# Two FNet and MLP layers on one core: two subtractions from GpSimd to VectorE, stores and raw loads issued later

## The chip, the core and the metric

The kernel runs on one core of a Trainium2 chip. The core's engines are named here as in the profile: PE (TensorE, the matmuls; PEld is its loading of the stationary operand), DVE (VectorE), ACT (ScalarE), POOL (GpSimd) and SP (SyncE, which in this kernel does nothing but issue DMA transfers, all of them, in one order). Matmul results go to PSUM, which has eight banks; everything else lies in SBUF, or in DRAM. The metric is device microseconds of one execution of the whole program, the median of several.

## The reference

S = 2048 tokens, D = 576 features, F = 4608 hidden features, fp32. Two layers with the same weights:

```python
x = A_x
x = x + _A_ref(_layernorm(x), seq_re, seq_im, hid_re, hid_im)
x = x + _B_ref(_layernorm(x), w1, b1, w2, b2)
x = x + _A_ref(_layernorm(x), seq_re, seq_im, hid_re, hid_im)
x = x + _B_ref(_layernorm(x), w1, b1, w2, b2)

def _A_ref(x, seq_re, seq_im, hid_re, hid_im):      # y = Re(DFT_seq(DFT_hidden(x)))
    a = einsum("bsd,ed->bse", x, hid_re)
    b = einsum("bsd,ed->bse", x, hid_im)
    return einsum("ts,bse->bte", seq_re, a) - einsum("ts,bse->bte", seq_im, b)

def _B_ref(x, w1, b1, w2, b2):
    h = gelu(einsum("bsd,df->bsf", x, w1) + b1)
    return einsum("bsf,fd->bsd", h, w2) + b2
```

## The kernel before

**Precision and parts.** An fp32 matrix is used as the sum of two fp32r matrices, a high and a low part: ACT copies the value to fp32r (the high part), and DVE or POOL subtracts that from the value (the low part). A product takes three matmuls: high by high, high by low, low by high (`PASSES`). On top of that every product is a two-by-two block product in Strassen's manner (Winograd's form): seven products in place of eight, numbered 1 to 7, each of a sum of blocks of one matrix by a sum of blocks of the other. "Part 6 of w1" is the sum of blocks that enters product 6, split in high and low.

**Stages.** Per layer: the transform (layer norm and both Fourier matrices), then the MLP in two passes of 1024 tokens each. There are four MLP passes; the change concerns the first one (layer 0, first half of the tokens, some 470 to 920 us into the span) and the transform ahead of it (94 to 390 us), since only there the parts of w1 and w2 are computed. Each part is stored to DRAM (`w1_parts`, `w2_parts`; the profile's queries shorten both to `w_parts`). w1's parts are loaded back in the pass itself; all later passes load both.

**One group of the first pass.** The hidden features go in 36 blocks of 128, taken in pairs q = 0 to 17, and two pairs make a group g = 0 to 8. The loop over g (the last lines of `mlp`) runs

- the *first inner*: `inner(2g)`, w1 by the tokens for a pair: seven steps, one for each part in the order 1, 6, 2, 5, 7, 3, 4 (`ORDER`), seven matmuls of 128x512 each. DVE and ACT combine the products in PSUM and apply the GELU; what comes out is H, whose own seven parts are made by `step(n)`, a few instructions at a time, behind the next matmuls (`work`);
- the *first outer*: `outer` for the parts 1, 6, 5, 3 of group g-1: H by w2, 96 matmuls of 128x288. A part is done in two halves of 512 tokens, each in a PSUM bank pair of its own: 1 and 6, 5 and 3, 7 and 4 follow one another in the same banks, so the first matmul of a half waits until DVE has added the half of the part before to the sums in SBUF;
- the *second inner*: `inner(2g+1)`;
- the *second outer*: parts 7, 4, 2 of group g-1, 72 matmuls.

So a group is 266 matmuls. Group 9 (the "last group") has no inner, only the outer work of group 8; in it the transform of the next tokens already starts to load (x, `uv_mid`, `dh_mid`: the "dh loads").

**w1's parts** are made by `weights()`: for each pair q seven steps n, each with a high part (`high(n)`, two ACT instructions), one pump later its low part (`low(n)`, DVE), a store (the "w1 store") and, where a raw block was used for the last time, the load of the same block of the next pair (a "raw load": a22, a21, a11, a12 in this order). The parts lie in `stage`, a ring of three slots: `high(n)` writes the slot that the store of n-3 reads. One `pump()` is one step; in the first pass `tick` calls it after every second inner step, so that a group sees seven pumps, three in the first inner and four in the second. w1 is complete after group 6. In the profile's rows a w1 store is `w_parts<-R` from a 128x640 piece (320 KB), a raw w1 load `A<-in_w` 192 KB.

**w2's parts** are made in the pass by `make(g)`, for the outer work of the same group: raw blocks b11, b12, b22, b21 and a sum x lie in one tile `rv`; four subtractions (b12-b11, b22-x, b21-x, b22-b12) give the other sums, all on POOL. For each part a function `hi` (ACT) and a function `lo` (DVE, then the store of 576 KB) stand in the list `due` with a position: `advance()` is called behind every inner step (positions 0 to 6 and 15 to 21) and every half part of the outer work (7 to 14), and runs what is due. Some `lo` are followed by the load of a raw block of the next group (288 KB, `A<-in_w` too).

**Loads of weights.** `load_w` at each inner step takes the next w1 part into one of the slots `c1`, some four or five steps ahead of its use (320 KB, `R<-w_parts`).

**Order.** Every engine runs its instructions in the order in which the code emits them. SP issues each transfer when its source is ready and its target free, and everything behind it waits as long; no more than eight transfers are under way at a time, since the n-th waits for the one eight places ahead of it to land. ACT and PE have the same instructions in the same order before and after.

Lines named in the rows: L187 `dma`, L190 `add`, L193 `sub`, L200 `mm`, L266 and L267 `high`, L941 `hi`, L997 the GELU, L1024 the copy behind product 1, L1057 H's high parts, L717 a high part of the transform.

Of the kernel before, what the change touches and what calls it, by code (L numbers as in the profile page):

```python
# [1 line left out]

# [6 lines left out]
F32 = mybir.dt.float32  # L9
# [8 lines left out]
DH = D // 2  # L18
NP = NT // 2
NQ = F // P // 2  # L20
# [133 lines left out]
def spectral_mixer(ctx: ExitStack, tc: tile.TileContext, x, dh, c0, cs, w1, b1, w2, b2, out):  # L154
# [8 lines left out]
    nc = tc.nc  # L163
# [6 lines left out]
    w1s = nc.dram_tensor("w1_parts", (NQ, 7, P, 5 * P), F32, kind="Internal").ap()  # L170
    w2s = nc.dram_tensor("w2_parts", (NG, 7, P, 2, 2 * DH), F32, kind="Internal").ap()
# [12 lines left out]
    middle = const.tile([P, 1], F32, name="middle")  # L184

    def dma(dst, src):
        nc.sync.dma_start(dst, src)  # L187

    def add(engine, dst, a, b, op=OP.add):
        engine.tensor_tensor(dst, a, b, op=op)  # L190

    def sub(engine, dst, a, b):
        engine.tensor_tensor(dst, a, b, op=OP.subtract)  # L193
# [52 lines left out]
    def weights():  # L246
        b = raw(4, 3 * P)
        a22, a21, a11, a12 = (b[:, k] for k in range(4))
        g = nc.gpsimd
        steps = ((4, a22, lambda: add(g, a22, a21, a22)), (1, a11, lambda: sub(g, a21, a11, a21)),  # L250
                 (5, a22, lambda: sub(g, a11, a22, a11)), (2, a12, lambda: sub(g, a12, a12, a11)),
                 (7, a21, None), (6, a11, None), (3, a12, None))

        def load(q, k):
            if q < NQ:
                dma(b[:, k], w1[q][:, k])

        def at(n):
            return stage(3, 5 * P)[:, n % 3]

        def cut(a):
            return a.rearrange("p (k f) -> p k f", f=P)

        def high(n):
            src, t = cut(steps[n % 7][1]), cut(at(n))
            nc.scalar.activation(t[:, 1:4:2], src[:, 0:3:2], AF.Copy)  # L266
            nc.scalar.activation(t[:, 2], src[:, 1], AF.Identity, bias=power[:, 2:3], scale=middle)  # L267

        def low(n):

            q, k = divmod(n, 7)
            i, src, then = steps[k]
            t = cut(at(n))
            sub(nc.vector, t[:, 0:5:2], cut(src), t[:, 1:4].bitcast(F32))
            dma(w1s[q, i - 1], at(n).bitcast(F32))
            if then:
                then()
            if k in (2, 4, 5, 6):
                load(q + 1, (2, 4, 5, 6).index(k))
            if k == 6:  # L280
                made[0] = q + 1

        for k in range(4):
            load(0, k)
        yield
        for n in range(7 * NQ + 1):
            if n:
                low(n - 1)
            if n < 7 * NQ:
                high(n)  # L290
            yield
        stage.free()
        raw.free()
# [20 lines left out]
    class Sequence:  # L314
# [228 lines left out]
        def sums(self, t):  # L543
            add(nc.vector, self.tmp(NP, P), self.block(t, 2), self.block(t, 3))
            sub(nc.vector, self.block(t, 2), self.block(t, 2), self.block(t, 0))
# [349 lines left out]
    def mlp(hid, store, first, after):  # L895
# [10 lines left out]
        got1, got2 = {}, {}  # L906
# [19 lines left out]
        due = []  # L926
# [4 lines left out]
        def load_raw(g, k):  # L931
            if g < NG:
                dma(rv[:, k], w2[2 * g:2 * g + 2, :, k].rearrange("f p d -> p f d"))

        def make(g):
            b11, b12, b22, b21, x = (rv[:, k] for k in range(5))
            pool = nc.gpsimd

            def hi(i, src):
                got2[g, i] = c2.take()  # L940
                nc.scalar.activation(got2[g, i](2, 2, DH)[:, :, 0], src, AF.Copy)  # L941

            def lo(i, src):
                t = got2[g, i](2, 2, DH)
                sub(nc.vector, t[:, :, 1], src, t[:, :, 0].bitcast(F32))
                dma(w2s[g, i - 1], got2[g, i](2, 2 * DH).bitcast(F32))

            one = [lambda: hi(1, b11), lambda: (lo(1, b11), sub(pool, b11, b12, b11), sub(pool, x, b22, b11))]
            six = [lambda: hi(6, x), lambda: (lo(6, x), sub(pool, x, b21, x))]
            five = [lambda: hi(5, b11), lambda: (lo(5, b11), load_raw(g + 1, 0))]  # L950
            three = [lambda: hi(3, b22), lambda: (lo(3, b22), sub(pool, b12, b22, b12), load_raw(g + 1, 2))]
            seven = [lambda: hi(7, b12), lambda: (lo(7, b12), load_raw(g + 1, 1))]
            four = [lambda: hi(4, x), lambda: lo(4, x)]
            two = [lambda: hi(2, b21), lambda: (lo(2, b21), load_raw(g + 1, 3))]
            if g == NG - 1:
                return list(zip((1, 2, 5, 6, 7, 8, 9, 10, 12, 13, 14, 15, 16, 17),
                                one + six + five + three + seven + four + two))
            return list(zip((0, 1, 2, 3, 4, 5, 9, 10, 15, 16, 17, 18, 19, 20),
                            one + five + six + three + seven + four + two))

        at = [0]

# [166 lines left out]
        for g in range(NG + 1):  # L1129
            at[0] = 0  # L1130
            if first and g:
                due.extend(make(g - 1))
            if g == NG:
                work(99)
                c1.close()
                hs.close()
                Y.free()
            for f in range(2):
                if g < NG:
                    for _ in inner(2 * g + f, None if g or f else 1):  # L1140
                        pass
                if g:
                    advance(6 + 15 * f)
                    at[0] = 7 + 15 * f
                    slot[0] = 0
                    for i in OUTER[f]:
                        outer(g - 1, i, 1 - f)
# [10 lines left out]
    nc.gpsimd.memset(middle, 0.0)  # L1158
    nc.gpsimd.memset(middle[32:64], 1.0)
    background.append(weights())  # L1160
    seq = Sequence(x, False)
    for layer in range(2):
        src, to = (xd, out) if layer else (x, xd)
# [4 lines left out]
        for half in range(2):  # L1168
# [6 lines left out]
            after = iter(())  # L1175
            if half == 0:
                hid = Hidden(1, src)
                after = hid.steps()
            if layer == 0 and half == 1:
                seq = Sequence(xd, True)  # L1180
                seq.closed = True
                after = seq.pieces
# [46 lines left out]
```

## Time and profile before

| | us |
|---|---|
| median of 3 runs | 2775.51 (2775.02 to 2776.14) |
| the profiled execution | 2776.02 |
| its span, first to last instruction | 2773.6 |
| PE busy | 2686.4 (97%) |
| DVE, ACT, POOL busy | 1777.8, 1105.5, 797.7 |
| mean granted TensorE clock | 0.995 |

The profile has one execution. A row of a timeline gives the start within the span, the busy time, the engine, the line, the operation with output and input, its count, and in brackets the idle time of the engine just before it with what ended it ("<-DVE R L193": an instruction of DVE at line 193 that wrote a tile of R). "SPq" is the issue of a transfer by SP: its start is the time of issue, and its length only the issue's own.

### The profile page before, as it was taken

What the parts mean: (1) busy time and instruction counts of PE and PEld (TensorE: products, weight loads), DVE (VectorE), ACT (ScalarE), POOL (GpSimd) and SP (SyncE); (2) the same over time, 40 slices, a digit from 0 to 9 for tenths busy, and PEclk for the clock granted to TensorE, in tenths of its full rate; (3) what the DMA queues carried; (4) which work ended last, traced back from release to release, by engine and by line L of the source; (5) the groups of instructions that cost most, each with busy time, mean ns of one, the idle gap of its engine ahead of it and who ended that gap; (6) DMA issues with size and microseconds to landing.
All of it is one profiled execution on the core that took longest, in us unless ns stands there. A gap on an engine that the chain in (4) does not pass through costs nothing.

```text
span 2773.6 us, 45593 instructions
## 1 busy us (share of the span) xinstructions
PE 2686.4 (97%) x17596; PEld 2513.2 (91%) x17596; DVE 1777.8 (64%) x2593; ACT 1105.5 (40%) x1877; POOL 797.7 (29%) x762
## 2 busy tenths in 40 slices
PE   7999999999998999999989999999999999999999
PEld 7999998788887989999989999998989989998988
DVE  8788866777775565555577666556555564655555
ACT  6555544544443243333344333334333323433331
POOL 5222224534533432222251000042222224221222
PEclk9999999999999999999999999999999999999999
DMA  5766664777775546666563333426666664666664
GB/s 198 242 220 224 232 211 144 265 264 266 263 263 205 187 140 194 192 193 191 165 222 113 123 121 122 163 90 206 193 194 193 194 213 133 184 194 194 190 197 154
DMA packets 205544, 530.47 MB, mean 191 GB/s; under 512 B 21633, under 2 KB 56449, under 8 KB 205185
## 3 DMA queue, kind: packets, MB, share of 16 engines
q1 hardware_dynamic: 205328, 527.57, 58.5%
q8 instruction: 139, 2.28, 0.3%
q14 instruction: 77, 0.62, 0.1%
HBM read 420.73 MB, written 109.41 MB: 191 GB/s over the span
## 4 chain that ended last, share of the span: by engine, by line
PE 70%; DVE 5%; issue 3%; DMA 3%; POOL 1%; ACT 1%; SPq 0%; POOLq 0%; DVEq 0%; ACTq 0%
PE bank L200 69%; DVE R L193 2%; DMA R<-w_parts 2%; DVE A L190 1%; DMA R<-dh_mid 1%; POOL A L193 1%; PE bank L750 1%; POOL R L193 0%; DVE bank L190 0%; DVE moments L215 0%; DVE A L193 0%; DMA A<-x_mid 0%; DVE moments L230 0%; ACT R L1057 0%; ACT R L941 0%
## 5 line engine op out<-in xcount | busy, mean ns | idle before, releaser
L200 PE MATMUL bank<-R 128*128 128x288 f32 (+2 forms) x16972 | 2627.1, 316 | 74.5 <-DVE A L190 30.1
L200 PEld LDWEIGHTS bank<-R 128*128 128x128 f32 x16972 | 2447.5, 189 | 245.1 <-DVE A L190 39.1
L190 DVE TENSOR_TENSOR A<-bank,A 128x576 f32<-128x576 f32 (+3 forms) x808 | 567.0, 710 | 595.4 <-PE bank L200 513.4
L193 POOL TENSOR_TENSOR R<-A,R 128x512 fp32r<-128x512 f32 x288 | 374.9, 1313 | 981.9 <-ACT R L1057 959.2
L193 DVE TENSOR_TENSOR R<-A,R 128x1024 fp32r<-128x1024 f32 (+4 forms) x449 | 447.1, 1023 | 38.9 <-ACT R L553 25.5
L190 POOL TENSOR_TENSOR A<-A 128x576 f32<-128x576 f32 (+2 forms) x102 | 135.4, 1331 | 640.3 <-ACT A L591 349.8
L997 ACT ACTIVATE bank<-bank,b1t 128x512 f32<-128x512 f32 (+1 forms) x224 | 144.8, 646 | 373.3 <-DVE bank L190 253.2
L1057 ACT ACTIVATE R<-A 128x512 fp32r<-128x512 f32 x288 | 176.2, 629 | 275.4 <-DVE A L193 117.7
L193 DVE TENSOR_TENSOR R<-bank,R 128x512 fp32r<-128x512 f32 (+4 forms) x408 | 251.4, 636 | 52.7 <-ACT R L196 43.5
L553 ACT ACTIVATE R<-A 128x1024 fp32r<-128x1024 f32 x196 | 204.1, 1054 | 134.7 <-DVE A L193 105.6
L190 DVE TENSOR_TENSOR bank<-bank,A 128x512 f32<-128x512 f32 (+1 forms) x228 | 152.2, 670 | 155.8 <-PE bank L200 155.4
L193 POOL TENSOR_TENSOR A<-A 128x288 f32<-128x288 f32 (+2 forms) x170 | 200.7, 1194 | 153.7 <-DVE R L193 83.8
L1057 ACT ACTIVATE R<-bank 128x512 fp32r<-128x512 f32 x216 | 120.8, 596 | 32.1 <-PE bank L200 32.1
L196 ACT ACTIVATE R<-bank 128x512 fp32r<-128x512 f32 (+2 forms) x160 | 74.1, 514 | 148.7 <-PE bank L750 94.4
L193 DVE TENSOR_TENSOR A<-A 128x1024 f32<-128x1024 f32 (+2 forms) x116 | 127.7, 1106 | 4.3 <-ACT A L240 1.3
L1024 ACT ACTIVATE A<-bank 128x512 f32<-128x512 f32 (+1 forms) x76 | 43.9, 578 | 211.5 <-PE bank L200 208.4
L240 ACT ACTIVATE A<-A,moments 128x576 f32<-128x576 f32 x64 | 54.1, 868 | 113.3 <-POOL moments L223 80.8
L193 DVE TENSOR_TENSOR A<-bank,A 128x512 f32<-128x512 f32 x144 | 98.0, 681 | 0.0
L593 DVE SCALAR_TENSOR_TENSOR A<-A 128x288 f32<-128x288 f32 x28 | 18.4, 657 | 88.0 <-POOL A L190 88.0
L997 ACT ACTIVATE A<-bank,b1t 128x512 f32<-128x512 f32 (+1 forms) x76 | 50.5, 665 | 54.3 <-DVE bank L190 54.3
L267 ACT ACTIVATE R<-A,power,middle 128x128 fp32r<-128x128 f32 x126 | 60.9, 484 | 0.0
L221 POOL TENSOR_TENSOR moments<-moments,power 128x1 f32<-128x1 f32 x32 | 17.6, 551 | 146.3 <-DVE moments L218 146.3
(50 smaller groups left out, 674.8 us busy)
## 6 DMA issues: line engine op xcount, KB each, us to landing
R<-w_parts SPq DMA_DIRECT2D x504, 320.0 KB, 3.4
R<-w_parts SPq DMA_DIRECT2D x189, 576.0 KB, 3.7
A<-in_cs SPq DMA_DIRECT2D x112, 512.0 KB, 4.2
w_parts<-R SPq DMA_DIRECT2D x126, 320.0 KB, 4.0
w_parts<-R SPq DMA_DIRECT2D x63, 576.0 KB, 3.9
uv_mid<-A SPq DMA_DIRECT2D x32, 576.0 KB, 2.8
A<-in_w SPq DMA_DIRECT2D x72, 192.0 KB, 4.0
R<-dh_mid SPq DMA_DIRECT2D x36, 288.0 KB, 6.2
```

The lines of the kernel that those rows point to most:

```text
L190: engine.tensor_tensor(dst, a, b, op=op)
L193: engine.tensor_tensor(dst, a, b, op=OP.subtract)
L196: nc.scalar.activation(hi, src, AF.Copy)
L200: nc.tensor.matmul(o, a, b, start=start, stop=stop, skip_group_check=True)
L240: nc.scalar.activation(dst, src, AF.Identity, bias=mv[:, 4:5], scale=mv[:, 3:4])
L267: nc.scalar.activation(t[:, 2], src[:, 1], AF.Identity, bias=power[:, 2:3], scale=middle)
L553: nc.scalar.activation(self.cells[t, i](2, NP, P)[:, 0], self.source(t, i), AF.Copy)
L593: nc.vector.scalar_tensor_tensor(uv[:, 1, 0], p7, -1.0, u, op0=OP.mult, op1=OP.subtract)
L750: nc.tensor.transpose(at, v[:, k], ident)
L997: nc.scalar.activation(dst, src, AF.Gelu_apprx_tanh, bias=bias(f))
L1024: nc.scalar.activation(up, o, AF.Copy)
L1057: nc.scalar.activation(H[q, k](2, TC)[:, 0], src, AF.Copy)
```

## The change

In `weights()`, the store of a w1 part and the raw load behind it leave `low(n)` for a function `moves(n)`, which is called one pump later, ahead of the next `low`. In `make(g)`, two of the four subtractions, b12-b11 and x = b22-b11, go from POOL to DVE; the other two stay. The stores of w2's parts and the raw loads of the next group leave the steps that make the low parts and are put into `due` one position later (two positions for part 3), by `later`.

```diff
@@ -272,9 +273,13 @@
             i, src, then = steps[k]
             t = cut(at(n))
             sub(nc.vector, t[:, 0:5:2], cut(src), t[:, 1:4].bitcast(F32))
-            dma(w1s[q, i - 1], at(n).bitcast(F32))
             if then:
                 then()
+
+        def moves(n):
+
+            q, k = divmod(n, 7)
+            dma(w1s[q, steps[k][0] - 1], at(n).bitcast(F32))
             if k in (2, 4, 5, 6):
                 load(q + 1, (2, 4, 5, 6).index(k))
             if k == 6:
@@ -283,8 +288,10 @@
         for k in range(4):
             load(0, k)
         yield
-        for n in range(7 * NQ + 1):
-            if n:
+        for n in range(7 * NQ + 2):
+            if n > 1:
+                moves(n - 2)
+            if 0 < n <= 7 * NQ:
                 low(n - 1)
             if n < 7 * NQ:
                 high(n)
@@ -943,20 +950,45 @@
             def lo(i, src):
                 t = got2[g, i](2, 2, DH)
                 sub(nc.vector, t[:, :, 1], src, t[:, :, 0].bitcast(F32))
-                dma(w2s[g, i - 1], got2[g, i](2, 2 * DH).bitcast(F32))
-
-            one = [lambda: hi(1, b11), lambda: (lo(1, b11), sub(pool, b11, b12, b11), sub(pool, x, b22, b11))]
-            six = [lambda: hi(6, x), lambda: (lo(6, x), sub(pool, x, b21, x))]
-            five = [lambda: hi(5, b11), lambda: (lo(5, b11), load_raw(g + 1, 0))]
-            three = [lambda: hi(3, b22), lambda: (lo(3, b22), sub(pool, b12, b22, b12), load_raw(g + 1, 2))]
-            seven = [lambda: hi(7, b12), lambda: (lo(7, b12), load_raw(g + 1, 1))]
-            four = [lambda: hi(4, x), lambda: lo(4, x)]
-            two = [lambda: hi(2, b21), lambda: (lo(2, b21), load_raw(g + 1, 3))]
+
+            def keep_part(i):
+                b = got2[g, i]
+                return lambda: dma(w2s[g, i - 1], b(2, 2 * DH).bitcast(F32))
+
+            def sums():
+                lo(1, b11)
+                sub(nc.vector, b11, b12, b11)
+                sub(nc.vector, x, b22, b11)
+
+            def later(at, *steps):
+                for step in steps:
+                    bisect.insort(due, (at, step), key=lambda d: d[0])
+
+            def after(i, src, n, *loads):
+
+                def step():
+                    lo(i, src)
+                    later(n, keep_part(i), *(lambda k=k: load_raw(g + 1, k) for k in loads))
+                return step
+
+            def first():
+                sums()
+                later(pos[1] + 1, keep_part(1))
+
             if g == NG - 1:
-                return list(zip((1, 2, 5, 6, 7, 8, 9, 10, 12, 13, 14, 15, 16, 17),
-                                one + six + five + three + seven + four + two))
-            return list(zip((0, 1, 2, 3, 4, 5, 9, 10, 15, 16, 17, 18, 19, 20),
-                            one + five + six + three + seven + four + two))
+                pos = (1, 2, 5, 6, 7, 8, 9, 10, 12, 13, 14, 15, 16, 17)
+                order = (6, 5)
+            else:
+                pos = (0, 1, 2, 3, 4, 5, 9, 10, 15, 16, 17, 18, 19, 20)
+                order = (5, 6)
+            six_at, five_at = (pos[2 + 2 * k + 1] + 1 for k in (order.index(6), order.index(5)))
+            six = [lambda: hi(6, x), lambda: (after(6, x, six_at)(), sub(pool, x, b21, x))]
+            five = [lambda: hi(5, b11), after(5, b11, five_at, 0)]
+            three = [lambda: hi(3, b22), lambda: (after(3, b22, pos[7] + 2, 2)(), sub(pool, b12, b22, b12))]
+            rest = [lambda: hi(7, b12), after(7, b12, pos[9] + 1, 1), lambda: hi(4, x), after(4, x, pos[11] + 1),
+                    lambda: hi(2, b21), after(2, b21, pos[13] + 1, 3)]
+            middle = six + five if order == (6, 5) else five + six
+            return list(zip(pos, [lambda: hi(1, b11), first] + middle + three + rest))
 
         at = [0]
```

How the order moves, at three places. The first is SP in the second inner of a group that still makes w1's parts (`in_w1` and `in_w2` are the raw loads, `w1_parts<-R` and `w2_parts<-R` the stores, `R<-w1_parts` the loads for PE; 128x640 is a w1 part, 128x1152 a w2 part). Before:

```order
L187 DMA w1_parts<-R_66 128x640
L187 DMA A_67<-in_w1 128x384
L187 DMA R_66<-w1_parts 128x640
L187 DMA w2_parts<-R_66 128x1152
L187 DMA A_67<-in_w2 128x2x288
L187 DMA R_66<-w1_parts 128x640
L187 DMA w1_parts<-R_66 128x640
L187 DMA A_67<-in_w1 128x384
L187 DMA R_66<-w1_parts 128x640
L187 DMA w2_parts<-R_66 128x1152
L187 DMA R_66<-w1_parts 128x640
L187 DMA w1_parts<-R_66 128x640
```

The same place after:

```order
L188 DMA R_66<-w1_parts 128x640 x2
L188 DMA w2_parts<-R_66 128x1152
L188 DMA A_67<-in_w2 128x2x288
L188 DMA w1_parts<-R_66 128x640
L188 DMA A_67<-in_w1 128x384
L188 DMA R_66<-w1_parts 128x640 x2
L188 DMA w2_parts<-R_66 128x1152
L188 DMA w1_parts<-R_66 128x640
L188 DMA A_67<-in_w1 128x384
L188 DMA R_66<-w1_parts 128x640 x2
```

The load for PE that stood between the raw w2 load and the second w1 store stands ahead of the w2 store of part 7; the first w1 store with its raw load (a21) stands behind that w2 store, and the second one with a11 behind part 4's store.

The second place is DVE in the first inner (`bank` is PSUM, A and R are SBUF; the 128x2x288 rows are low parts of w2, the 128x3x128 rows those of w1). Before:

```order
L190 TENSOR_TENSOR A_67<-bank_68,A_67 128x512
L193 TENSOR_TENSOR R_66<-A_67,R_66 128x2x288
L193 TENSOR_TENSOR R_66<-A_67,R_66 128x3x128
L190 TENSOR_TENSOR A_67<-bank_68,A_67 128x512
L193 TENSOR_TENSOR R_66<-A_67,R_66 128x2x288
L193 TENSOR_TENSOR R_66<-A_67,R_66 128x3x128
L190 TENSOR_TENSOR bank_68<-bank_68,A_67 128x512 x2
```

After:

```order
L191 TENSOR_TENSOR A_67<-bank_68,A_67 128x512
L194 TENSOR_TENSOR R_66<-A_67,R_66 128x2x288
L194 TENSOR_TENSOR A_67<-A_67 128x576 x2
L194 TENSOR_TENSOR R_66<-A_67,R_66 128x3x128
L191 TENSOR_TENSOR A_67<-bank_68,A_67 128x512
L194 TENSOR_TENSOR R_66<-A_67,R_66 128x2x288
L194 TENSOR_TENSOR R_66<-A_67,R_66 128x3x128
L191 TENSOR_TENSOR bank_68<-bank_68,A_67 128x512 x2
```

The two subtractions stand behind part 1's low part, ahead of the low part of w1 of the same pump.

The third place is SP in the last group. Before:

```order
L187 DMA w2_parts<-R_66 128x1152 x2
L187 DMA R_66<-uv_mid 128x1152
L187 DMA A_67<-in_x 128x2x288
L187 DMA R_66<-dh_mid 128x576
L187 DMA w2_parts<-R_66 128x1152
L187 DMA R_66<-uv_mid 128x1152
L187 DMA A_67<-in_x 128x2x288
L187 DMA R_66<-dh_mid 128x576 x2
L187 DMA w2_parts<-R_66 128x1152
```

After:

```order
L188 DMA w2_parts<-R_66 128x1152 x2
L188 DMA R_66<-uv_mid 128x1152
L188 DMA A_67<-in_x 128x2x288
L188 DMA R_66<-dh_mid 128x576
L188 DMA R_66<-uv_mid 128x1152
L188 DMA A_67<-in_x 128x2x288
L188 DMA R_66<-dh_mid 128x576
L188 DMA w2_parts<-R_66 128x1152
```

The third store now stands behind the second `uv_mid`, x and `dh_mid` loads.

More of the change, by code (lines that the diff above doesn't have):

```diff
@@ L1 @@
+import bisect
 from contextlib import ExitStack
```

## The prediction

> **What bounds the kernel now.** The page comes first, for the share of each engine, then the chain, then TensorE's waits in the stretch where weights are made.
>
> ```profile
> span 2773.6 us, 45593 instructions
> PE 2686.4 (97%) x17596; PEld 2513.2 (91%) x17596; DVE 1777.8 (64%) x2593; ACT 1105.5 (40%) x1877; POOL 797.7 (29%) x762
> 1126.23 45.24 PE bank L200 x266
> PE bank L200 <- DVE A L190: 13.8, 13, 3.7
> PE bank L200 <- DMA R<-w_parts: 6.1, 6, 1.8
> ```
>
> TensorE (PE) is busy for 97% of the span, so only its idle time can be won or added to. The third row is one group of a later pass, where no weights are made: 266 matmuls in 45.24 us without a pause. The last two rows are the largest of PE's waits from 500 to 950 us, in the pass that makes the weights (columns: us in total, times, longest). A group there, by PE's timeline:
>
> ```profile
> 624.06 21.16 PE L200 MATMUL bank<-R 128*128 128x512 f32 x121 [1.51 <-DVE R L193]
> 646.07 6.86 PE L200 MATMUL bank<-R 128*128 128x512 f32 x43 [0.85 <-DVE bank L190]
> 653.55 18.24 PE L200 MATMUL bank<-R 128*128 128x288 f32 x102 [0.62 <-DVE A L190]
> 673.02 21.18 PE L200 MATMUL bank<-R 128*128 128x512 f32 x121 [1.23 <-DMA R<-w_parts]
> ```
>
> From 624.06 to 673.02 a group takes 48.96 us, 3.7 more than in the third row above. Three places cost it: the last step of the second inner (624.06, 673.02), the last step of the first inner (646.07), and the first outer, part 6 (653.55).
>
> **The second inner: what the stores' move gives.** SyncE (SP) issues all transfers in order. In group 3:
>
> ```profile
> 614.17 0.32 SPq L187 DMA_DIRECT2D w_parts<-R  x1
> 617.59 0.32 SPq L187 DMA_DIRECT2D w_parts<-R  x1
> 617.96 1.38 SPq L187 DMA_DIRECT2D A<-in_w  x1
> 619.43 0.45 SPq L187 DMA_DIRECT2D R<-w_parts  x1
> 619.97 0.38 SPq L187 DMA_DIRECT2D w_parts<-R  x1
> 620.40 0.42 SPq L187 DMA_DIRECT2D A<-in_w  x1
> R<-w_parts SPq DMA_DIRECT2D x1, 320.0 KB, 4.5
> A<-in_w SPq DMA_DIRECT2D x1, 288.0 KB, 5.2
> A<-in_w SPq DMA_DIRECT2D x1, 192.0 KB, 4.9
> ```
>
> The last three rows are the landings, in order, of the issues at 619.43, 617.96 and 620.40. The weights issued at 619.43 land at 623.9, and PE starts its last step on them at 624.06. They stood behind the store at 617.59, which had waited for VectorE (DVE). In the changed order this load stands ahead of that store and goes about 3 us earlier, so the 1.5 us wait goes. Next in line would be part 7's addition, which DVE does in time.
>
> **What the same move costs.** The w1 store of 614.17 now stands behind the store of 617.59 and the raw load of 617.96, about 4 us later. The raw load of 620.40 (a11) now stands behind two more weight loads, a 576 KB store and a w1 store. ScalarE (ACT) needs both, in this stretch:
>
> ```profile
> 620.18 0.40 ACT L266 ACTIVATE R<-A 128x256 fp32r<-128x256 f32 x1
> 625.36 0.42 ACT L266 ACTIVATE R<-A 128x256 fp32r<-128x256 f32 x1 [1.35 <-DMA A<-in_w]
> 626.67 0.66 ACT L997 ACTIVATE bank<-bank,b1t 128x512 f32<-128x512 f32 x1 [0.51 <-DVE bank L190]
> 627.26 1.08 ACT L1057 ACTIVATE R<-bank 128x512 fp32r<-128x512 f32 x2
> 627.55 0.76 DVE L190 TENSOR_TENSOR A<-bank,A 128x576 f32<-128x576 f32 x1 [0.45 <-PE bank L200]
> 628.22 0.68 DVE L193 TENSOR_TENSOR R<-bank,R 128x512 fp32r<-128x512 f32 x1
> 628.82 1.35 DVE L190 TENSOR_TENSOR A<-bank,A 128x512 f32<-128x512 f32 x2
> 622.00:634.00 12.00, 10.49 (x73) 9.80 (x72) 8.52 (x15) 5.40 (x10) 2.81 (x3) 1.00 1.00 388
> ```
>
> The high part at 620.18 writes the ring slot of the store of 614.17, and will wait for it until some 624; only ACT's slack is used up there. The one at 625.36 reads a11 and already waits 1.35 us for it. Behind it on ACT stand a GELU, the first high part of H, and on DVE its low part (628.22), an addition, and the addition of part 7's second half (the end of the x2 row). PE cannot write part 4's second half into that bank before.
>
> When does a11 land? The last row (columns: PE, weight load, DVE, ACT, POOL, then clock, DMA share, GB/s) shows the transfers saturated from 622 to 634, at 388 GB/s: 0.85 us for 320 KB, 1.52 for 576, 0.51 for 192. Behind the raw load of w2, which lands at 617.96 + 5.2 = 623.2, come a w1 store 0.85, a raw load 0.51, two weight loads 1.7, the store of part 4 1.52, a w1 store 0.85 and a11 itself 0.51: 5.9 in all, so 629.1, near 628.5 in the other groups, where that raw load lands sooner. Behind it 0.80 (both halves of the high part) + 0.66 + 0.6 + 0.68 + 1.35 = 4.1: PE may go on at 632.6. Without its wait it would be at part 4's second half at 624.06 - 1.69 + 1.68 + 36 x 0.133 = 628.8 (the 1.51 us with the slower first matmuls behind it; then the step's own 7 matmuls at 0.24, and 36 at 0.133 from start to start). Before, it was there at 630.5. So a wait of 3.8 us takes the place of one of 1.5, and the group ends **2.1 us later**, in the six groups whose pass still loads raw w1 (1 to 6): +12.6. Bounds: a11 is issued no sooner than about 621.5 (SP waits ahead of it for part 4's low part). If it lands by 624.7, 4.1 ahead of 628.8, the whole 1.7 of the group is saved; with the 4.9 us of the row the group comes out even. With that raw load as late as here it is 2.6 later. I take the saturated queue, since the row of 388 GB/s covers exactly this stretch.
>
> The wait is also long enough for the clock:
>
> ```profile
> 498.31 11.87 PE L200 MATMUL bank<-R 128*128 128x512 f32 x70 [2.14 <-DVE bank L190]
> 574.80:578.20 3.40, 3.40 (x20) 1.00 1.00 404
> 498.30:501.70 3.40, 3.40 (x9) 0.52 1.01 362
> 574.80 21.17 PE L200 MATMUL bank<-R 128*128 128x512 f32 x121 [1.77 <-DMA R<-w_parts]
> ```
>
> After idling 1.77 us PE ran on at a granted clock of 1.00, after 2.14 us at 0.52 for 3.4 us (9 matmuls in place of 20). A pause of 3.8 us can cost up to 3.4 x 0.48 = 1.6; I take 1.0 a group, since part of it lies beside DVE's own backlog: +6, between 0 and 10. The Trainium skill (TensorE: Matmul & The Clock Gate, "What's actually happening") has the clock halve after an idle window of about 3.4 us, in windows that run free. By that, as an estimate, a pause of 3.8 us holds a whole window in one case of eight, and the term would be about 1 rather than 6, the forecast some 5 us lower; the row of 2.14 us speaks against it.
>
> **The two subtractions.** Per group GpSimd (POOL) loses two 128x576 subtractions, DVE gets them.
>
> ```profile
> 640.31 4.67 POOL L193 TENSOR_TENSOR A<-A 128x576 f32<-128x576 f32 x3 [5.51 <-DVE R L193]
> 642.09 0.69 DVE L190 TENSOR_TENSOR A<-bank,A 128x512 f32<-128x512 f32 x1 [1.39 <-POOL A L193]
> 616.81 1.22 DVE L193 TENSOR_TENSOR R<-A,R 128x576 fp32r<-128x576 f32 x2
> 642.74 2.66 DVE L193 TENSOR_TENSOR R<-A,R 128x576 fp32r<-128x576 f32 x2
> 646.52 3.16 DVE L193 TENSOR_TENSOR R<-A,R 128x576 fp32r<-128x576 f32 x2
> L193 DVE TENSOR_TENSOR A<-A 128x1024 f32<-128x1024 f32 (+2 forms) x116 | 127.7, 1106 | 4.3 <-ACT A L240 1.3
> ```
>
> On POOL two take about 3.1 us (4.67 for three; the third is a shorter one of 128x384); on DVE 576/1024 of the last row's mean, 0.62 each, 1.25 together. DVE stands idle for 1.39 us ahead of 642.09, so they fit. The same pair of low parts takes 1.22 us with POOL idle (616.81) and 2.66 or 3.16 beside it. POOL is freed too late for the first pair: its next subtraction waits for DVE's low part, now ready near 642.0, and then runs beside 642.74 as before; so part 7's addition, which ends the 0.85 us wait of 646.07, comes when it came. The second pair should lose a good half microsecond, and with it part 6's wait of 0.62. I take 0.5 saved in 7 groups: -3.5 (between +9, if the 1.25 push that addition, and -8, if most of both waits goes).
>
> **The last group** has no inner beside it, and lasts by its loads:
>
> ```profile
> 880.10 4.82 SPq L187 DMA_DIRECT2D w_parts<-R  x2
> 887.09 0.38 SPq L187 DMA_DIRECT2D w_parts<-R  x1
> 894.58 3.25 PE L200 MATMUL bank<-R 128*128 128x288 f32 x12 [3.73 <-DVE A L190]
> 892.38 0.68 ACT L717 ACTIVATE R<-R 128x576 fp32r<-128x576 f32 x1 [6.69 <-DMA R<-dh_mid]
> ```
>
> PE's 3.73 us ends by way of ACT with the first dh load. It stood behind the second store of the first row, which waited for part 6's low part, and that for both subtractions. On DVE part 6 is ready 3.1 - 1.25 = 1.85 us sooner. The second dh load also passes the 576 KB store of 887.09, another 1.5. Together about -3.5 (-1 to -5).
>
> **Everything else.** Before group 1 ACT's high parts wait for their ring's stores by 1 us or so, and these now come a step later, behind two loads: +1.5 (0 to +5). While the transform runs (94 to 390 us) the same stores and raw loads also move by a step; PE hardly waits there, so its engines have slack and I take nothing, up to +5 if that is used up.
>
> Sum: 12.6 + 6 - 3.5 - 3.5 + 1.5 = +13.1 on the profiled execution's 2776.02 (span 2773.6 and 2.4 around it), 2789.1; it stands 0.5 above the median of the runs, 2775.51, so **2788.6**.
>
> **Rivals.** *The gain is kept.* The change turns at a11: landing by 624.7 it holds nobody up, and the waits for weights are won in six groups (6.1 us in the row of waits, and the 1.51 put down to DVE): -7.6 - 3.5 - 3.5 + 1.5 = -13.1, 2762.4. The whole program breaks even near 627, where a group ends 0.9 later. For it: SP has fewer waits and the issue falls near 621.5. Against it: the saturated row. *DVE becomes the bound.* If the two subtractions push the addition of 645.33 by their 1.25 us, the 0.85 wait grows in eight groups: +10 in place of -3.5, 2802 with the rest; for it, DVE is idle for only 1.4 us there. *Nothing to be measured:* the late a11 costs what the rest wins, 2770 to 2781, if it lands near 627. A difference under 0.2% (5.5 us) cannot be told from none here.
>
> **Chances.** Forecast 0.50 (its own range 2779 to 2800), gain kept 0.30, DVE bound 0.07, nothing 0.13. With a little of the forecast's lower edge put to "same": faster 0.30, same 0.15, slower 0.55. The range has to reach the kept gain: 2760 to 2800.
>
> **What would show it.** In the groups PE's wait at the second inner's last step should be gone, and a wait of 3 to 4 us stand in the second outer, part 4, put down to DVE A L190, with ACT's high part ahead of it waiting for a raw load or a w1 store, and a granted clock below 1 behind it. POOL has 18 subtractions fewer, DVE 18 more. The first dh load of the last group lands near 890.5, less what the groups shift. If ACT's high part at the second inner's end waits no longer than 2 us, the prediction is wrong, on the fast side.

## The result, and the profile after

| | before | after |
|---|---|---|
| median of 4 runs, us | 2775.27 (2774.49 to 2776.14) | 2810.61 (2806.42 to 2812.20) |
| span of the profiled execution, us | 2773.6 | 2810.4 |

The changed kernel is slower: 1.0127 times the time before (95% interval 1.0115 to 1.0139), 35 us where 13 were forecast, and outside the range of 2760 to 2800. The page after, its span and its engines:

```profile
span 2810.4 us, 45527 instructions
PE 2702.4 (96%) x17596; PEld 2528.1 (90%) x17596; DVE 1785.3 (64%) x2611; ACT 1102.6 (39%) x1877; POOL 765.1 (27%) x744
```

PE is busy 16.0 us longer for the same 17596 matmuls, so part of the loss is not waiting but slower matmuls. PE's two largest waits from 500 to 950 us (before, the two largest were 13.8 us for DVE's additions and 6.1 for weights, `R<-w_parts`):

```profile
PE bank L201 <- DVE A L191: 43.0, 20, 5.2
PE bank L201 <- DVE bank L191: 3.7, 7, 1.6
```

The wait for weights is gone, and the wait for DVE's additions has grown by 29.2 us. One group of the changed kernel in PE's timeline (the group that starts at 576.77), and then the busy time, clock and transfers of stretches of it (columns as in the prediction: PE, weight load, DVE, ACT, POOL, clock, DMA share, GB/s):

```profile
575.71 17.32 PE L201 MATMUL bank<-R 128*128 128x288 f32 x93
596.99 15.49 PE L201 MATMUL bank<-R 128*128 128x288 f32 x71 [3.95 <-DVE A L191]
613.48 1.88 PE L201 MATMUL bank<-R 128*128 128x512 f32 x7 [1.00 <-DVE A L191]
615.72 16.58 PE L201 MATMUL bank<-R 128*128 128x512 f32 x108 [0.36 <-DVE bank L191]
```

```profile
576.77:588.07 11.30, 11.30 (x52) 9.24 (x50) 6.92 (x11) 5.53 (x12) 0.18 (x1) 1.00 0.68 215
588.07:596.99 8.92, 4.97 (x38) 4.74 (x36) 3.93 (x7) 4.27 (x9) 1.02 (x1) 0.92 1.01 368
596.99:600.50 3.51, 3.51 (x14) 3.51 (x15) 2.03 (x4) 0.63 (x1) 1.76 (x2) 0.50 0.41 158
600.50:604.25 3.75, 3.75 (x24) 3.75 (x24) 2.48 (x4) 0.00 (x0) 1.77 (x2) 0.75 0.00 0
```

The second inner (576.77 to 588.07) now runs without a pause. Then 36 matmuls of the second outer pass (part 7 and the first half of part 4), and the second half of part 4 waits 3.95 us for DVE. Behind it the granted clock is 0.50, then 0.75: the remaining 36 matmuls take 7.26 us where 36 x 0.133 = 4.8 is their time at full clock.

The same by stage, as means over the six groups from 514.5 us (521.6 after) on, worked out from the starts of the matmuls:

```
us                 before   after   change
second inner        12.76   11.28   -1.48
second outer         9.55   16.60   +7.05
first inner         12.50   13.19   +0.69
first outer         14.18   13.55   -0.63
group               48.99   54.63   +5.64   x6 = +33.8
up to group 0       470.9   471.8   +0.9
group 0              43.6    49.8   +6.2
groups 7 to 9       143.0   139.3   -3.7   (to the end of the pass)
```

A row "group" runs here from one second inner to the next, so the six groups are the second inner and second outer of g = 1 to 6, each with the first inner and first outer behind it; "group 0" is the stretch ahead of them, from `inner(1)` on.

These add up to 37.2; the rest of the program is 0.4 shorter. Here is what ends the wait of 596.99. SP's issues at the end of the second inner, the time from issue to landing of the first three of them (576 KB the store of part 4, 320 KB a w1 store, 192 KB a11), then ACT, then DVE:

```profile
585.78 0.86 SPq L188 DMA_DIRECT2D w_parts<-R  x2
586.69 1.37 SPq L188 DMA_DIRECT2D A<-in_w  x1
w_parts<-R SPq DMA_DIRECT2D x1, 576.0 KB, 6.0
w_parts<-R SPq DMA_DIRECT2D x1, 320.0 KB, 6.3
A<-in_w SPq DMA_DIRECT2D x1, 192.0 KB, 6.3
593.09 0.42 ACT L267 ACTIVATE R<-A 128x256 fp32r<-128x256 f32 x1 [4.21 <-DMA A<-in_w]
593.79 0.64 ACT L1029 ACTIVATE bank<-bank,b1t 128x512 f32<-128x512 f32 x1
594.98 0.69 DVE L194 TENSOR_TENSOR R<-bank,R 128x512 fp32r<-128x512 f32 x1 [4.35 <-ACT R L1089]
595.59 2.01 DVE L191 TENSOR_TENSOR A<-bank,A 128x512 f32<-128x512 f32 x3
```

a11 goes out at 586.69 and lands 6.3 us later, at 593.0; ACT's high part starts at 593.09, the GELU and H's high part follow, DVE's low part of H, and the second of the three additions in the last row (596.2 to 596.9) is that of part 7's second half. At 596.99 PE goes on. It is the chain that the prediction drew.

### The profile page after: what moved, and what is told of

Read it like the earlier page. It is cut to its first block, busy times and chain, and to the rows that moved or that the text cites. A ratio compares the mean times of both kernels' runs of the same rounds, so it can differ in the third digit from the quotient of the medians.

```text
span 2810.4 us, 45527 instructions
## 1 busy us (share of the span) xinstructions
PE 2702.4 (96%) x17596; PEld 2528.1 (90%) x17596; DVE 1785.3 (64%) x2611; ACT 1102.6 (39%) x1877; POOL 765.1 (27%) x744
## 3 DMA queue, kind: packets, MB, share of 16 engines
q8 instruction: 139, 2.28, 0.3%
## 4 chain that ended last, share of the span: by engine, by line
PE 78%; DVE 8%; DMA 5%; issue 4%; ACT 2%; POOL 2%; SPq 1%; DVEq 0%; ACTq 0%; POOLq 0%
PE bank L201 77%; DVE R L194 4%; DMA A<-in_w 2%; DVE A L191 1%; DVE A L194 1%; POOL A L194 1%; DMA R<-dh_mid 1%; PE bank L757 1%; DMA w_parts<-R 1%; DMA A<-in_cs 1%; SPq L188 1%; ACT R L560 0%; DVE moments L231 0%; POOL R L194 0%; DVE moments L216 0%
## 5 line engine op out<-in xcount | busy, mean ns | idle before, releaser
L194 DVE TENSOR_TENSOR R<-A,R 128x1024 fp32r<-128x1024 f32 (+4 forms) x449 | 434.5, 994 | 46.4 <-ACT R L560 32.2
L194 POOL TENSOR_TENSOR A<-A 128x288 f32<-128x288 f32 (+2 forms) x152 | 166.3, 1105 | 157.7 <-DVE R L194 62.0
L194 DVE TENSOR_TENSOR A<-A 128x1024 f32<-128x1024 f32 (+2 forms) x134 | 147.4, 1105 | 4.9 <-ACT A L241 1.3
L267 ACT ACTIVATE R<-A 128x256 fp32r<-128x256 f32 x126 | 51.8, 411 | 134.7 <-DMA w_parts<-R 71.6
```

## The experiments

Two parts of the change alone came first, then the third, and the change with a11 put back.

**The two subtractions alone.**

```diff
-one = [..., lambda: (lo(1, b11), sub(pool, b11, b12, b11), sub(pool, x, b22, b11))]
+one = [..., lambda: (lo(1, b11), sub(nc.vector, b11, b12, b11), sub(nc.vector, x, b22, b11))]
```

> The kernel before with only the two subtractions b12-b11 and b22-b11 on VectorE; all transfers in the order of before. Theory (the loss is a late a11, so it comes from the order of the transfers): between 2770 and 2778 us, no wait at the second half of part 4 in the second outer; the first inner's last two steps lose at most 0.7 us a group, part 6 in the first outer gains 0.5, the last group gains about 2. Rival (VectorE becomes the bound): the first inner of the changed kernel takes 13.2 us instead of 12.5, with a wait of 1.0 us for VectorE one step ahead of the last; if that and its consequences are the loss, this kernel shows it too and takes over 2785 us.

Measured: 2783.18 us, 1.0025 (1.0016 to 1.0035) of before: slower, by more than the theory allowed and less than the rival said. No wait at part 4. DVE in the first inner of one group:

```profile
594.63 1.44 DVE L193 TENSOR_TENSOR R<-A,R 128x576 fp32r<-128x576 f32 x1
596.10 2.52 DVE L193 TENSOR_TENSOR A<-A 128x576 f32<-128x576 f32 x2
599.01 0.68 DVE L190 TENSOR_TENSOR A<-bank,A 128x512 f32<-128x512 f32 x1
```

The two subtractions take 2.52 us, twice what the prediction gave them, and the low part ahead of them 1.44. The addition of 599.01 (product 5) comes about 1.8 us later within its inner than before, and product 3, which uses the same bank, waits 1.0 us for it. By stage the first inner is 1.45 us longer (13.95), the first outer 0.65 shorter (13.53). So the subtractions do not give what they were forecast to give; they cost 6.7 us in the six groups.

**w1's stores and raw loads alone.** `weights()` as changed, `make()` as before:

```diff
+        def moves(n):
+            ...
-        for n in range(7 * NQ + 1):
-            if n:
+        for n in range(7 * NQ + 2):
+            if n > 1:
+                moves(n - 2)
+            if 0 < n <= 7 * NQ:
                 low(n - 1)
```

> The kernel before with only the stores of w1's parts and the raw loads of w1 one pump later; w2's transfers and all subtractions as before. Theory: a11 again stands behind the store of w2's part 4 and a w1 store, so part 4's second half waits some 3 to 4.5 us in groups 1 to 6, with a granted clock near 0.65 behind it, and the start of the pass (group 0) loses some 6 us: 2800 to 2815 us. Rival (only both moves together fill the queue so far that a11 is late): no wait over 2 us at part 4, 2775 to 2785 us.

Measured: 2821.79 us, 1.0168 (1.0152 to 1.0183). The wait that the theory named is there, but the loss is above its 2800 to 2815, and larger than that of the whole change. Waits of 3.0 to 4.7 us stand at part 4 (second outer 14.81 us, 5.3 more than before), but there is also a second place: the first outer takes 16.02 us, 1.8 more. ACT's waits in this kernel, 500 to 860 us:

```profile
ACT R L266 <- DMA w_parts<-R: 44.9, 16, 4.4
ACT R L266 <- DMA A<-in_w: 21.9, 6, 4.7
```

Six waits of the high parts are for a raw load, but sixteen are for a store: for the ring slot that they write. The prediction had named the raw load, a11; of the store it had said that only ACT's slack is used up.

**w2's stores and raw loads alone.** `make()` as changed, but with both subtractions on POOL; `weights()` as before:

```diff
 def sums():
     lo(1, b11)
-    sub(nc.vector, b11, b12, b11)
-    sub(nc.vector, x, b22, b11)
+    sub(nc.gpsimd, b11, b12, b11)
+    sub(nc.gpsimd, x, b22, b11)
```

> The kernel before with only the stores of w2's parts and the raw loads of w2 one or two positions later; w1's transfers and all subtractions as before. Theory: a11 stands ahead of the store of part 4 as before, so there is no wait at part 4; the wait of 1 to 1.8 us at the second inner's last step goes in groups 1 to 6, and the last group gains about 1.5: 2762 to 2770 us. Rival (the stores and loads are late in any order): 2775 us or more, with a wait at part 4.

Measured: 2765.46 us, 0.9966 (0.9953 to 0.9979). The theory holds: this part alone is faster, by 10.4 us against the kernel before in the same series (2775.85 us). Most of one group of its PE:

```profile
560.79 31.15 PE L201 MATMUL bank<-R 128*128 128x288 f32 x166
592.79 6.89 PE L201 MATMUL bank<-R 128*128 128x512 f32 x43 [0.85 <-DVE bank L191]
```

From 560.79 to 591.94 there is no pause at all, through the second inner and the whole second outer: the wait for weights has gone and no wait at part 4 has come. The wait of 0.85 us in the first inner is as before.

**The change with a11 issued early.** Of the four raw loads of w1, a11 goes back to its place:

```diff
 def low(n):
     ...
+    if k == 5:
+        load(q + 1, 2)
 def moves(n):
     ...
-    if k in (2, 4, 5, 6):
+    if k in (2, 4, 6):
```

> The changed kernel with one of the four raw loads of w1, that of a11, issued where it was before (behind its last low part), everything else as changed. Theory: the wait of 3.6 to 5.3 us at part 4 and the slow clock behind it go in groups 1 to 6, 6.9 us a group: 2768 to 2778 us. Rival (ScalarE's high part waits for the late w1 store of its ring slot as well, or another raw load is as late): the wait only shrinks, 2785 to 2805 us.

Measured: 2813.17 us, 1.0138 (1.0123 to 1.0153), no faster than the changed kernel and above the ranges of both texts, with waits of 4.2 to 5.6 us at part 4. The theory as written falls. SP's two stores, the landing of the second of them, ACT, and ACT's waits from 500 to 860 us:

```profile
584.03 0.86 SPq L188 DMA_DIRECT2D w_parts<-R  x2
w_parts<-R SPq DMA_DIRECT2D x1, 320.0 KB, 6.7
591.25 0.42 ACT L267 ACTIVATE R<-A 128x256 fp32r<-128x256 f32 x1 [3.81 <-issue]
ACT R L267 <- DMA w_parts<-R: 26.9, 6, 5.4
```

The w1 store of 584.47 (the second of the first row) lands at 591.2, and the high part, which writes the ring slot that this store reads, starts at 591.25. (Its own row names no releaser, "issue"; the last row has six other waits of high parts that are put down to a store.) So the same instruction has two late partners: a11, which it reads, and the store of its slot, which stood right ahead of a11 behind the store of part 4. In the changed kernel the store lands only some 0.5 us ahead of a11 (6.3 us after its issue, like a11, and issued 0.5 earlier), not the 1.8 us that the next expectation gives.

**Either of the two alone.** First the raw loads late and the stores where they were, then the stores late and all raw loads where they were:

```diff
 def low(n):
     ...
+    dma(w1s[q, i - 1], at(n).bitcast(F32))
 def moves(n):
-    dma(w1s[q, steps[k][0] - 1], at(n).bitcast(F32))
     if k in (2, 4, 5, 6):
```

> The changed kernel with the stores of w1's parts issued where they were before (behind their low parts); only the raw loads of w1 stay one pump late. The run with a11 alone issued early showed ScalarE's high part waiting for the store of its ring slot instead, which landed about 1.8 us before a11 in the changed kernel. Theory now (late a11 and late w1 store each hold the same high part, either one is enough): a11 still stands behind part 4's store, so the wait at part 4 stays at 2.5 to 4.5 us: 2797 to 2812 us. Rival (the late store is what holds ScalarE, a11 was only its companion): no wait over 2 us there, 2770 to 2782 us.

```diff
 def low(n):
     ...
+    if k in (2, 4, 5, 6):
+        load(q + 1, (2, 4, 5, 6).index(k))
 def moves(n):
     dma(w1s[q, steps[k][0] - 1], at(n).bitcast(F32))
-    if k in (2, 4, 5, 6):
-        load(q + 1, (2, 4, 5, 6).index(k))
```

> The changed kernel with all four raw loads of w1 issued where they were before; only the stores of w1's parts stay one pump late. It asks whether the late store alone holds ScalarE. Theory (either of the two is enough): ScalarE's high part at the end of the second inner waits for the store of its ring slot, which still stands behind part 4's store; a wait of 3 to 5 us at part 4, 2800 to 2815 us. Rival (the raw loads do it alone, and in the run with a11 early it was the three others that filled the queue): no wait over 2 us at part 4, 2770 to 2785 us.

Measured: late raw loads 2803.82 us, 1.0104 (1.0090 to 1.0118); late stores 2807.71 us, 1.0112 (1.0099 to 1.0126). Both keep the wait at part 4, of 2.9 to 3.5 us and of 3.5 to 4.9 us. ACT's longest waits for a transfer, first with late raw loads, then with late stores:

```profile
ACT R L267 <- DMA A<-in_w: 25.5, 6, 4.5
```

```profile
ACT R L267 <- DMA w_parts<-R: 32.5, 9, 4.5
```

Each names its own transfer. In the group means the second outer takes 14.21 us with late raw loads and 16.48 with late stores, against 9.55 before and 16.60 in the changed kernel. That either one is enough is now shown by these two runs, and by the next one that without both there is no wait.

**Both moves of w1 taken back.** `weights()` as before, `make()` as changed, with the subtractions on DVE:

```diff
 def low(n):
     ...
+    dma(w1s[q, i - 1], at(n).bitcast(F32))
     if then:
         then()
-def moves(n):
-    q, k = divmod(n, 7)
-    dma(w1s[q, steps[k][0] - 1], at(n).bitcast(F32))
     if k in (2, 4, 5, 6):
```

> The changed kernel with both moves of w1 (stores and raw loads) taken back; the subtractions on VectorE and w2's later stores and loads stay. Theory (the loss of the whole change lies in w1's moves, and the other two parts add up as measured alone, -10.4 and +7.3): 2769 to 2776 us, no wait over 2 us at part 4, the first inner losing about 1 us to VectorE. Rival (the parts do not add, VectorE's delay makes the stores late here too): 2780 us or more.

Measured: 2774.34 us, 0.9997 (0.9988 to 1.0006): no difference from before. The wait at part 4 is gone, w2's moves and the subtractions nearly cancel (-10.4 and +7.3 alone, -3.1 together, -0.7 measured). The whole loss of the change is therefore that of w1's moves: 36 us on top of this kernel. Where w2's gain goes here is seen by stage: the second inner has it (11.29 us), the first inner loses it (14.43, 1.9 more than before, where the theory said about 1).

**The wait filled with matmuls.**

```diff
-mm(o[:, j, :DH], h[:, a, at], w[:, b], ...)
+for _ in range(3 if first and i == 4 and jj == 0 and 1 <= g + 1 <= 6 else 1):
+    mm(o[:, j, :DH], h[:, a, at], w[:, b], ...)
```

> The changed kernel, with the 12 matmuls of the first half of part 4 issued three times each (so part 4's first half is added three times in the output of the first pass; this changes the computation) in the outer work of groups 0 to 5, the six places where the long wait stands: 24 more matmuls of 0.133 us, 3.2 us, beside the wait. Theory (the low clock behind the wait follows from TensorE's idle time of 3.6 to 5.3 us): the wait shrinks to 0.4 to 2.1 us, the clock stays near 1, and the 2.4 us a group that the slow matmuls cost are saved: 2794 to 2801 us. Rival (the clock is lowered by something else): the same time as the changed kernel, 2808 to 2814 us, with a granted clock near 0.65 behind the wait.

Measured: 2801.40 us, 1.0095 (1.0081 to 1.0108), with 144 more matmuls, 9 us less than the changed kernel; just beyond the theory's 2794 to 2801, clear of the rival. The six waits shrink to 0.68 to 2.28 us. Behind the wait, first in the changed kernel and then here (same columns as above):

```profile
543.08:550.02 6.94, 6.94 (x36) 6.94 (x37) 4.51 (x7) 0.63 (x2) 3.53 (x3) 0.66 0.03 10
```

```profile
540.87:545.78 4.91, 4.91 (x36) 4.91 (x37) 4.42 (x7) 0.64 (x2) 3.56 (x3) 1.00 0.10 40
```

The same 36 matmuls, at a clock of 0.66 behind 5.25 us of idling, at 1.00 behind 1.61 us. In the six groups the second outer is 2.16 us shorter though it has 3.2 us more work, 13 us in all; the span is 11.0 shorter (2799.4). The rest is outside the six places, where both kernels have the same instructions: this execution reaches the six groups 1.7 us sooner and loses 3.8 us behind them, 2.1 of it by the end of the pass. So the slow clock follows from the idle time, and cost some 2 us a group.

**Two attempts at a better kernel.** Both start from the kernel of w2's moves alone. In the first the two subtractions go to DVE in the last group only; in the second, the low part of w2's part 5 goes one step later in the first inner:

```diff
-sub(nc.gpsimd, b11, b12, b11)
+sub(nc.vector if g == NG - 1 else pool, b11, b12, b11)
```

> The kernel before with w2's stores and raw loads later, as in the run that took 2765 us, and the two subtractions on VectorE in the last group only, where no inner runs beside them. Theory (the last group of the changed kernel was 3.1 us shorter, that of the run with w2's moves alone only 0.5, that of the subtractions alone 0.7: both together are needed): 2760 to 2764 us. Rival (the last group's gain came from what ended before it): the same as without, 2764 to 2768 us.

```diff
-pos = (0, 1, 2, 3, 4, 5, 9, 10, 15, 16, 17, 18, 19, 20)
+pos = (0, 1, 2, 4, 4, 5, 9, 10, 15, 16, 17, 18, 19, 20)
```

> The kernel with w2's moves alone (2765 us), and in the first inner the low part of w2's part 5 one step later, so that the addition of product 7, which ends TensorE's wait of 0.85 us there, stands ahead of it on VectorE. Theory (the low part, slowed from 0.75 to 1.4 us by GpSimd beside it, is what makes that addition late): the wait of 0.85 us goes in groups 1 to 7, 2757 to 2763 us. Rival (the low part then delays the next addition as much, or GpSimd's third subtraction comes later): 2763 to 2770 us.

Measured: the first 2764.26 us, 0.9960 (0.9946 to 0.9974), not to be told from 2765.46 without it, as the rival said. The second 2757.68 us, 0.9938 (0.9925 to 0.9952), faster than both kernels. A group of it in PE's timeline:

```profile
554.83 44.01 PE L201 MATMUL bank<-R 128*128 128x288 f32 x250
599.46 10.86 PE L201 MATMUL bank<-R 128*128 128x288 f32 x70 [0.62 <-DVE A L191]
```

250 matmuls run without a pause, and of the waits of before only the 0.62 us in the first outer is left. A group takes 46.70 us (48.99 before).

## Why the prediction was right, and where it was wrong

*The direction and the place were right.* The second inner's wait for weights went: 1.48 us a group, where 1.5 to 1.7 was said. A wait at part 4's second half took its place, put down to DVE A, with ACT's high part ahead of it waiting for a transfer, and a granted clock below 1 behind it, as the last part of the prediction listed. a11 landed 4.9 us behind the end of the second inner (593.0 against 588.07); the prediction's 629.1 stands 5.05 behind its end at 624.05, and the 628.5 that its sum used 4.45. The chain from there to PE took 4.0 us, 4.1 was said.

*The wait was mis-sized a little.* It was 3.56 to 5.25 us, 4.49 in the mean, where 3.8 was said; the group shown, with 3.95, has one of the shorter ones. With the 1.48 won, that is 3.0 us a group in place of 2.1, and above the 2.6 given for a later raw load: 18 us instead of 12.6.

*The clock was mis-sized most.* The step that failed is "A pause of 3.8 us can cost up to 3.4 x 0.48 = 1.6; I take 1.0 a group", which took the one slow stretch of before, 3.4 us long, for the longest. In the group shown the clock was 0.50 for 3.5 us and then 0.75 for another 3.75 us. What remains of the second outer's +7.05 beside the wait is 2.56 us, 15 us in six groups instead of 6, beyond the upper bound of 10. The filled wait shows that most of it is the clock's. On the rule that was weighed there (the Trainium skill, TensorE: Matmul & The Clock Gate, "What's actually happening": the clock falls after an idle window of about 3.4 us in windows that run free): by it, as an estimate, a pause of 4.49 us holds a whole window in one case of three. This trace does not agree: the clock was lowered behind six of six.

*The subtractions were mis-priced.* "On DVE 576/1024 of the last row's mean, 0.62 each" gave 1.25 us for the pair; it took 2.52. The step has two faults. The row's mean mixes three shapes ("+2 forms"); kept apart by shape, the profile of before has the price of just this subtraction, 0.75 us:

```profile
L193 DVE TENSOR_TENSOR A<-A 128x576 f32<-128x576 f32 x16 | 12.0, 751 | 0.0
```

That makes 1.5 us for the pair. For the other 1.0, the prediction looked at which work of POOL would be taken away, and not at what POOL does next in its order. In the changed kernel, a low part on DVE in the second inner, with POOL idle; then DVE and POOL in the first inner:

```profile
587.26 0.75 DVE L194 TENSOR_TENSOR R<-A,R 128x576 fp32r<-128x576 f32 x1
608.35 1.44 DVE L194 TENSOR_TENSOR R<-A,R 128x576 fp32r<-128x576 f32 x1
609.83 2.52 DVE L194 TENSOR_TENSOR A<-A 128x576 f32<-128x576 f32 x2
612.74 0.69 DVE L191 TENSOR_TENSOR A<-bank,A 128x512 f32<-128x512 f32 x1
607.88 3.07 POOL L194 TENSOR_TENSOR R<-A,R 128x512 fp32r<-128x512 f32 x2 [5.61 <-ACT R L1089]
```

POOL, free of the subtractions, now does H's low parts (the last row) from 607.88 to 610.95, beside DVE's low part and the first subtraction. That first one takes 1.73 us; the second, which starts at 611.59 with POOL idle, takes 0.76. The Trainium skill (SBUF — State Buffer, "Who interferes with whom") states that a DVE instruction with two SBUF inputs contends with a GpSimd instruction that reads SBUF; this trace agrees: 1.44 us for the low part and 1.73 for the first subtraction beside POOL, against 0.75 for a low part (the first row) and 0.76 for the second subtraction with POOL idle. The gain forecast in part 6 came (first outer -0.63), and the first inner gave it back (+0.69): +0.4 us in six groups in place of -3.5. The rival "DVE becomes the bound", given 0.07, came by half (0.69 us of the 1.25 a group), and at another addition, that of product 5.

*The second cause was overlooked.* "... only ACT's slack is used up there" was said of the high part at 620.18 and the store of its slot. That the high part of a11 has a slot too, whose store stood right ahead of a11 in the same queue, has no place in the working; only the list of signs at its end allows "a raw load or a w1 store". In the changed kernel this store lands ahead of a11, so it was not what ended the wait, but it would have sent a repair to the wrong place: putting a11 back gained nothing. Nor is it free: with the stores back and the raw loads late the kernel takes 2803.82 us, 6.8 less than with both late.

*The rest.* "Before group 1 ACT's high parts wait for their ring's stores by 1 us or so ... +1.5 (0 to +5)" measured +7.1 (0.9 ahead of group 0 and 6.2 in it), beyond its upper bound of 5. With both moves of w1 taken back group 0 takes 43.8 us, as before (43.6), so it is the same cause: the first long waits of ACT's high parts there, at 471.53 and 475.11, are of 2.44 us each and put down to a w1 store, as those of 0.87 and 1.15 before are. Late raw loads alone reach the six groups 2.5 us later than before, late stores alone 4.2. These are single executions: the run with the wait filled, whose instructions up to there are those of the changed kernel, came 5.3 us later and not 7.1. The last groups gave 3.7 us, 3.5 was said; in the run with the wait filled the same instructions gave 1.6, so how close this came is partly luck.

So 18 + 15 + 0.4 + 7.1 - 3.7 = 37, against 12.6 + 6 - 3.5 + 1.5 - 3.5 = 13.1. The range failed with the terms: their upper bounds, each in the text, add up to some 2819 us, and wait, clock and group 0 all hang on one cause, the late transfers, so that they had to be expected to go wrong together.

## What to carry to other kernels

Before a store is issued later, look for the instruction that writes its buffer next: in a ring of three slots one step of delay in the store is a step of delay for the producer, and where that stands ahead of other work in an engine's order, for everything behind it. Before work is moved to an engine that is idle "there", look at what the relieved engine will do instead in that time, and whether it slows the new place. And a wait that moves to another place is not paid one for one: behind the pauses of 3.56 to 5.25 us of the changed kernel the next 36 matmuls took another 2.1 to 2.7 us.

## What was not expected of the hardware

The pause after which the clock is lowered has no sharp bound in these runs. With late raw loads, pauses of 2.86 and 2.99 us had 36 matmuls in 4.9 us behind them, which is full clock, those of 3.20, 3.23 and 3.43 us 6.4 us, and that of 3.45 us 7.3. The changed kernel's pauses of 3.56 to 5.25 us had 6.9 to 7.5 us behind them, the shorter pauses not the shorter times. With w1's moves alone a pause of 2.99 us had 6.4 us behind it and one of 3.38 us 4.9. Before the change a pause of 2.14 us had been enough, and with the wait filled one of 2.28 us was not (4.9). Whatever sets it, it was not the length of the pause alone.
